# Part of an MLP's second product moved behind the scheduled stage, and a tail of Strassen products in place of the output projection

## The chip, the cores and the metric

The kernel runs on one core of one Trainium2 chip. The metric is the device time of one execution in microseconds. A core has a matrix engine (TensorE, PE in the profile; its weight loads are PEld), VectorE (DVE), ScalarE (ACT), GpSimd (POOL) and SyncE (SP, which only issues DMAs here). Each runs its own list of instructions in order and waits on semaphores for the others.

## The reference

One token block of S = 2048 rows and D = 1024 columns; 32 heads of width 32; an MLP of 3584 inner columns.

```python
xn = layernorm(x)
q, k, v = split(xn @ wqkv)                       # 32 heads of 32
p = softmax(q @ k.T * 32 ** -0.5)                # 2048 x 2048 for each head
s = concat(p @ v) @ wo
h = xn @ w1 + b1                                 # 2048 x 3584
act = h * tanh(log1p(exp(-abs(h))) + max(h, 0))  # mish
g = silu(act @ w2)
out = x + s * g
```

All is f32. The outer products with weights are computed in TensorE's fp32r form: each operand is split into a high part and a low part (the rest), and a product is three matmuls, high by high, high by low, low by high (`THREE`). The split is an ACT copy to the high part (`copy`, L288) and a subtraction for the low part (`low`, L296).

## The kernel before

It has three stages.

1. Layer norm, transposes, v, and q and k. The q/k product is already done by Strassen's scheme: 7 products of half-size blocks in place of 8, with sums of blocks made on the vector engines (L798). Up to about 519 us.
2. The scheduled stage, to about 3179 us. Streams of operations (`t_stream`, `s_stream`, `h_stream`, `y_stream`, `p_stream`) give each operation an engine, a cost, a key (its due time, from `due`, `SLOW` and `UNTIL`) and what it takes from rings of buffers and PSUM banks. `Plan` lays them out one after another in a list scheduler, and that order is the order in which the instructions are written. The string `LEAN` chooses, stretch by stretch, which kinds lean forward. Numbers in it only set the order.
   For each of the 32 heads: the scores q·k are computed twice, once for their row maxima (`s`, L920, reduced on DVE, L926), once with the maximum in the contraction, for exp (`t`, L1007, then ACT, tile `p`, 128x2048 for each of 16 key tiles). The product p·v is made in groups of 6, 5 and 5 key tiles (`pv`, L1054). The denominators are a chain on POOL: 15 adds of 128x2048 into one tile `z` (L1036). After the last add, four column blocks of `z` are summed over the partitions by matmuls with ones (`zp`, L1080), and ACT and DVE make the reciprocal and scale the head's output, which is stored to `ot` in DRAM. The next head's `z` chain starts when the `zp` of the head before has read its `z`.
   Beside it runs the MLP, over 4 chunks of 512 rows and 28 inner tiles of 128 columns: `h` (L1213), mish on ACT and DVE (the operations `d1` to `d7`, `a1` to `a5`; `a5` and `d7` are the split of the activation), and the second product `y` (L1303), in blocks of two inner tiles (`YB`), whose partial results DVE adds into `yacc` (L1325). A chunk's `yacc` is stored to `ys`. The weights w2 are split once (ACT and POOL), kept in DRAM (`w2s`) and reloaded for each chunk.
3. The output projection, `op` (L1402): 768 matmuls, 16 row tiles x 2 halves x 8 x 3. `p_stream` prepares its weights (`wo`, in pieces of 128x1024) and first inputs within the scheduled stage; the first half of the sums for the first four row tiles is planned as the end of that stage. Each result is multiplied by silu(y) and added to x on DVE (L1495, L1496).

Of the kernel before, what the change touches and what calls it, by code (L numbers as in the profile page):

```python
# [40 lines left out]
PS, ACTS, W2S, Y0, Y1 = 7, 3, 5, 0.6, 0.17  # L41
# [11 lines left out]
LEAN = ("11875111088588544715468766661886741604280263056046486663654100588"  # L53
        "24308444562028442608686254255866647666488105044664767708017872000")
# [176 lines left out]
def body(ctx: ExitStack, tc: tile.TileContext, x, wqkv, wo, w1, b1, w2, out):  # L231
# [23 lines left out]
    ys = [dram.tile([P, 4, D], F32, name=f"ys{i}") for i in range(NC)]  # L255
    zeros = dram.tile([DH, S], F32R, name="zeros")
# [638 lines left out]
    total = 2 * 4 * NS * MM + NC * FT * 48 * MM + NS * PV  # L895
# [332 lines left out]
    def mish(n, made, t):  # L1228
# [51 lines left out]
        o5 = op("DVE", 0.69, need=[o4], emit=d5, give=[("d", p2), ("b", p2)], kind="mish")  # L1280
        o6 = op("DVE", 0.69, need=[o5, o3], emit=d6, give=["r"], kind="mish")
# [3 lines left out]
    w2_took, w2_uses, w2_ends = {}, {}, {}  # L1285
    yacc = mlp.tile([P, 4, D], F32, name="yacc")

    def y_stream():
        for m in range(W2S):
            w2_op(m, [m_there[0, 3]])  # L1290
        for B in range(NC * FT // YB):
            c, b = divmod(B, FT // YB)
            done = []
            for dh in range(2):
                for s in range(4):
                    t = {}
                    for j in range(YB):
                        n, m_ = YB * B + j, (B * 2 + dh) * YB + j
                        for i, (p, q) in enumerate(THREE):
# [10 lines left out]
                            due = YB * B + YB + Y0 + g * Y1 + (BEHIND if B >= NC * FT // YB - 2 else 0)  # L1310
# [6 lines left out]
                            if s == 3 and i == 2 and m_ + W2S < NC * FT * 2:  # L1317
                                w2_op(m_ + W2S)
# [9 lines left out]
            if b == FT // YB - 1:  # L1328
# [6 lines left out]
    wt, ohl, ps, wo_loads, wo_ops, o_ops, o_first = {}, {}, {}, {}, {}, {}, []  # L1335
    raws_ = {}

    def in_p(name):
        return lambda at: att.tile([P, S], F32, tag=f"p{at['p']}", name=name)

    def raw_op(name, halves, tile_of, loads, **kw):

        done = []
        for i, (n, src, from_) in enumerate(loads):
            def emit(at, i=i, n=n, src=src):
                if i == 0:
                    raws_[name] = tile_of(at)
                w = S // halves
                raws_[n] = raws_[name][:, i * w:(i + 1) * w]
                nc.sync.dma_start(raws_[n], src)  # L1350
            if i:
                kw = dict(need=done[:1])
            done.append(op("SP", 0.1, emit=emit, bytes_=P * S * 4 // halves,
                           **{**kw, "need": list(kw.get("need", ())) + from_}))
        return done

    def wo_raw(name, ks, tile_of, **kw):
        a = raw_op(name, 2, tile_of, [(("wo", k), wo[k * P:(k + 1) * P, :], []) for k in ks], **kw)
        for k, o in zip(ks, a):
            wo_loads[k] = o  # L1360

    def wo_op(k, where, eng, **kw):
        def high(at):
            wt[k] = where()
            copy(wt[k][:, 0], raws_["wo", k])

        def rest(at):
            low(nc.gpsimd if eng == "POOL" else nc.vector, wt[k][:, 1], raws_["wo", k], wt[k][:, 0])

        need = kw.pop("need", [])  # L1370
        a = op("ACT", 1.05, need=[wo_loads[k]] + need, emit=high, **kw)
        wo_ops[k] = op(eng, 2.36 if eng == "POOL" else 1.3, need=[a], emit=rest, key=2 * total if eng == "POOL" else None,
                       both=eng == "DVE")

    def o_raw(name, ks):
        a = raw_op(name, 4, in_p(name), [(("o", k), ot[k][:, 0:512], [stored[h] for h in range(4 * k, 4 * k + 4)])
                                         for k in ks], take=["p"])
        for k, o in zip(ks, a):
            o_op(k, o)

    def o_op(k, load):
        def high(at):
            if k % HK == 0:
                xts_.setdefault(NC, []).append(chunk("xo0", k // HK))
            ohl[0, k] = xts_[NC][k // HK][:, :, k % HK]
            copy(ohl[0, k][:, 0], raws_["o", k])

        a = op("ACT", 0.6, need=[load] + ([o_first[k // HK]] if k % HK else []),
               take=[] if k % HK else [f"xc{k // HK}"], emit=high)
        if k % HK == 0:  # L1390
            o_first.append(a)
        o_ops[k] = op("DVE", 0.69, need=[a], both=True,
                      emit=lambda at: low(nc.vector, ohl[0, k][:, 1], raws_["o", k], ohl[0, k][:, 0]))


    BANKS, bank_of = ("s", "s", "t", "t", "y", "y", "z", "o"), {}
# [8 lines left out]
    def p_stream():  # L1405
# [23 lines left out]
        while "h" not in final:  # L1429
            yield None  # L1430
# [130 lines left out]
```

## Time and profile before

| | |
|---|---|
| time, median of 3 runs | 3362.5 us (3362.36 to 3362.78) |
| span of the profiled execution | 3358.0 us |
| TensorE busy | 3345.8 us, 100% of the span |
| VectorE / ScalarE / GpSimd busy | 2510.8 / 2056.5 / 2524.7 us |
| matmuls of `y` (L1303) | 2688 |
| matmuls of `op` (L1402) | 768, in 174.11 us at the end |
| adds of `z` on POOL | 448 of 4615 ns and 32 of 4628 ns |

The time of a run is 4.5 us above the span of the profiled execution (3362.5 against 3358.0). The profile's page gives busy times by engine; groups of instructions by line; the chain of waits that ends last; and a timeline. TensorE's clock is full in all 40 slices of the span. A line number is that of the kernel before; lines in the changed kernel are 6 higher in the first parts (`low` is L302, the `z` add L1042, `zp` L1086), the tail's matmul is L1528 there, and its sums are L1375 (weights), L1414 (activations) and L1533 (results).

### The profile page before, as it was taken

How to read it: one execution, taken by the hardware profiler on the slowest of the kernel's cores; microseconds unless marked ns; L12 is line 12 of the kernel's file. 1: busy time of each engine (PE TensorE's matmuls, PEld its weight loads, DVE VectorE, ACT ScalarE, POOL GpSimd, SP SyncE). 2: the span in 40 equal slices, each digit the busy share in tenths (PEclk: the TensorE clock that was granted, in tenths of full speed). 3: DMA queues.
4: the chain of work that ended last, by engine and by line, in shares of the span. 5: the costliest groups of instructions: out<-in, count | busy, mean ns of one | idle time of the engine just before them, and what ended most of it. 6: DMA issues, size and time to landing. Idle time of an engine off the chain costs nothing.

```text
span 3358.0 us, 45795 instructions
## 1 busy us (share of the span) xinstructions
PE 3345.8 (100%) x16886; PEld 2458.4 (73%) x16886; DVE 2510.8 (75%) x3987; ACT 2056.5 (61%) x3313; POOL 2524.7 (75%) x750
## 2 busy tenths in 40 slices
PE   9999999999999999999999999999999999999999
PEld 7888887776777677776777677777677777767787
DVE  6665678877877778887888688888787888886542
ACT  5233436676766666666676666666667666667621
POOL 1323546999999887888888988888888898889800
PEclk9999999999999999999999999999999999999999
DMA  7865745454565643343335334333344433433482
GB/s 248 298 204 181 242 146 183 140 184 152 169 191 172 221 126 115 105 122 114 101 117 179 111 101 126 101 112 116 101 151 139 116 106 112 130 108 107 140 304 83
DMA packets 291460, 501.56 MB, mean 149 GB/s; under 512 B 88138, under 2 KB 151114, under 8 KB 269130
## 3 DMA queue, kind: packets, MB, share of 16 engines
q1 hardware_dynamic: 271524, 456.95, 43.8%
q10 hardware_dynamic: 19712, 41.69, 3.3%
q8 instruction: 133, 2.18, 0.3%
q14 instruction: 91, 0.75, 0.1%
HBM read 352.55 MB, written 144.97 MB: 148 GB/s over the span
## 4 chain that ended last, share of the span: by engine, by line
PE 96%; DMA 1%; DVE 1%; POOL 1%; issue 0%; ACT 0%; SPq 0%; ACTq 0%; POOLq 0%; DVEq 0%
PE y L1303 18%; PE h L1213 18%; PE t L1007 14%; PE s L920 13%; PE pv L1054 13%; PE op L1402 5%; PE v L354 5%; PE q_y L798 3%; PE q_z L798 2%; PE q_x L798 2%; PE zp L1080 1%; PE s L700 0%; POOL z L1036 0%; PE pt L423 0%; DMA w2r<-in_B_w_dram 0%
## 5 line engine op out<-in xcount | busy, mean ns | idle before, releaser
L1036 POOL TENSOR_TENSOR z<-z,p 128x2048 f32<-128x2048 f32 x448 | 2067.7, 4615 | 98.0 <-ACT p L285 72.9
L285 ACT ACTIVATE p<-t,zero 128x512 f32<-128x512 f32 x2048 | 1377.1, 690 | 560.1 <-PE t L1007 535.7
L926 DVE TENSOR_REDUCE mx<-s 128x1 f32<-128x512 f32 x1984 | 1322.3, 685 | 382.7 <-PE s L920 371.9
L1303 PE MATMUL y<-w,act 128*128 128x512 f32 x2688 | 920.3, 391 | 0.8 <-DVE yacc L1325 0.5
L1007 PE MATMUL t<-qstack,kstack 128*128 128x512 f32 x2048 | 799.1, 393 | 1.1 <-ACT p L285 0.7
L920 PE MATMUL s<-kstack,qstack 128*128 128x512 f32 x1984 | 772.6, 393 | 0.2 <-ACT p L285 0.2
L1213 PE MATMUL h<-xr,w 128*128 128x512 f32 x2016 | 697.7, 391 | 0.4 <-DMA xr<-xs 0.4
L1303 PEld LDWEIGHTS y<-w,act 128*128 128x128 f32 x2688 | 503.3, 188 | 114.3 <-issue 6.7
L1007 PEld LDWEIGHTS t<-qstack,kstack 128*128 128x128 f32 x2048 | 383.8, 188 | 114.8 <-issue 18.0
L1054 PE MATMUL pv<-p,v 128*32 128x512 f32 x4096 | 459.3, 594 | 0.0
L920 PEld LDWEIGHTS s<-kstack,qstack 128*128 128x128 f32 x1984 | 369.6, 188 | 118.5 <-issue 32.1
L1213 PEld LDWEIGHTS h<-xr,w 128*128 128x128 f32 x2016 | 378.3, 188 | 81.2 <-issue 3.4
L1325 DVE TENSOR_TENSOR yacc<-yacc,y 128x512 f32<-128x512 f32 x416 | 282.7, 680 | 82.6 <-PE y L1303 81.5
L1054 PEld LDWEIGHTS pv<-p,v 128*32 128x32 f32 x4096 | 123.3, 110 | 282.7 <-issue 281.1
L1036 POOL TENSOR_TENSOR z<-p,p 128x2048 f32<-128x2048 f32 x32 | 148.1, 4628 | 185.2 <-PE zp L1080 146.6
L1213 PE MATMUL h<-xc,w 128*128 128x512 f32 x672 | 231.3, 391 | 1.3 <-DMA w<-w1s 1.0
L354 PE MATMUL v<-vw,xc 128*128 128x512 f32 x768 | 179.7, 392 | 1.2 <-ACT xc L288 0.7
L354 PEld LDWEIGHTS v<-vw,xc 128*128 128x128 f32 x768 | 142.7, 188 | 32.0 <-ACT xc L288 1.4
L1213 PEld LDWEIGHTS h<-xc,w 128*128 128x128 f32 x672 | 125.9, 188 | 30.5 <-issue 2.5
L288 ACT ACTIVATE act<-h 128x512 fp32r<-128x512 f32 x112 | 66.6, 595 | 88.2 <-DVE h L1262 87.0
L798 PE MATMUL q_y<-xc,wq 128*128 128x512 f32 x480 | 115.3, 389 | 0.0
L798 PEld LDWEIGHTS q_y<-xc,wq 128*128 128x128 f32 x480 | 90.0, 188 | 18.8
(149 smaller groups left out, 2947.4 us busy)
## 6 DMA issues: line engine op xcount, KB each, us to landing
w<-w1s SPq DMA_DIRECT2D x91, 1024.0 KB, 5.4
w<-w2s SPq DMA_DIRECT2D x168, 512.0 KB, 4.0
w2s<-w SPq DMA_DIRECT2D x56, 512.0 KB, 4.0
qstack<-qs SPq DMA_DIRECT2D x96, 256.0 KB, 6.3
kstack<-ks SPq DMA_DIRECT2D x96, 256.0 KB, 5.8
w1s<-w SPq DMA_DIRECT2D x21, 1024.0 KB, 5.8
qs<-qst ACTq DMA_DIRECT2D x32, 512.0 KB, 4.1
ks<-qst ACTq DMA_DIRECT2D x32, 512.0 KB, 3.7
```

The source lines that it names most:

```text
L285: nc.scalar.activation(out_, in_, fn, bias=zero if bias is None else bias, scale=scale)
L354: nc.tensor.matmul(ps, xc[t // 4][k // HK][:, a, k % HK, (t % 4) * P:(t % 4 + 1) * P], vw[i, k // 2][:, b, k % 2], start=n == 0, stop=n == ...
L798: nc.tensor.matmul(ps, w[:, a, k], xx[:, b, k], start=m == 0 and i in (0, 1, 4), stop=m == 3 * HK - 1, skip_group_check=i not in (0, 1, 4))
L920: nc.tensor.matmul(sp_, qst[h % 3][:, qt * P:(qt + 1) * P], kst[h % 3][:, kc * 512:(kc + 1) * 512], start=True, stop=True)
L926: nc.vector.reduce_max(tiles["mx"][:, qt, kc:kc + 1], tiles[qt, kc], axis=AX.X)
L1007: nc.tensor.matmul(tp, kst[h % 3][:, kt * P:(kt + 1) * P], qst[h % 3][:, c * 512:(c + 1) * 512], start=True, stop=True)
L1036: nc.gpsimd.tensor_tensor(zs[h], pts[T - 1] if kt == 1 else zs[h], pts[T], ALU.add)
L1054: nc.tensor.matmul(pv[h][c * DH:(c + 1) * DH, :], vt[h][:, k, :], pts[T - kt + k][:, c * 512:(c + 1) * 512], start=k == 0, stop=k == NT - 1)
L1213: nc.tensor.matmul(t["h"], w1t[n][:, a, k], xts_[c][k // HK][:, b, k % HK], start=i == 0, stop=i == 3 * KT - 1)
L1303: nc.tensor.matmul(t["y"], acts[n][:, p, s * P:(s + 1) * P], w2t[m_][:, q], start=j == 0 and i == 0, stop=j == YB - 1 and i == 2)
L1325: nc.vector.tensor_tensor(ya, ya, t["y"], ALU.add)
L1402: nc.tensor.matmul(ps[t, dh], ohl[t // 4, k][:, a, s * P:(s + 1) * P], wt[k][:, b, r], start=k == 0 and i == 0, stop=k == KT - 1 and i == 2)
```

## The change

Eight of the 28 inner tiles (2, 5, 8, 11, 16, 19, 22, 25; `DEFER`) leave `y`. Their activations are not split but stored to DRAM (`ats`) by SP (`put`), after a mish that ends in `d6_`. `y` then runs over the 20 that are left, 10 blocks of two (`BLOCKS`). After the scheduled stage there is a tail of 16 jobs: eight "y" jobs make the share of the deferred tiles, for 256 rows each, and eight "o" jobs make the output projection for 256 rows each. Every job is a product of a 256x1024 by a 1024x1024 block by Strassen's scheme (Winograd's form): 7 products of half-size blocks (`mm7`), 12 matmuls each. The weights' four quarters b11, b12, b21, b22 (tiles `yb0` to `yb3` and `ob0` to `ob3`, 128x2048) give sums T1 to T4 and, split in high and low, seven units `yu0` to `yu6` (for the o jobs `ou0` to `ou6`). A job's inputs (`araw`) give sums S1 to S4 on POOL (in job 0 S1 and S2 on DVE) and seven units `a<job>_0` to `a<job>_6` of 128x512. Three PSUM banks x, y, z of a job take products 0 and 2, 1, 3 and 5, 4 and 6; `e<job>_0` is a copy of product 0 (ACT), that must be taken before product 2 is added to the same bank; `e<job>_1` and `e<job>_3` are DVE sums. "y" jobs add to `ys`, take silu and store to `gs`; "o" jobs load `gs` and x.

`tail_stream`, the last stream of the scheduled stage, loads the quarters into the buffers of the heads' stacks as these come free, and makes T3, T2, T4 and the lows of `yu0`, `yu1`, `yu2` on POOL and the first a-unit. The costs and order constants change too: `SLOW` 1.25 to 1.08, `Y1` 0.17 to 0.25, and another `LEAN`.

```diff
-SLOW, UNTIL = 1.25, 700.0
-W2_Q = 0
+SLOW, UNTIL = 1.08, 700.0
+DEFER = (2, 5, 8, 11, 16, 19, 22, 25)
+KEPT = [f for f in range(FT) if f not in DEFER]
+BLOCKS = [KEPT[i:i + 2] for i in range(0, len(KEPT), 2)]
+NB = len(BLOCKS)
+NP = NT // 2
...
+        if n % FT in DEFER:
+            o6 = op("DVE", 0.69, need=[o5, o3], emit=d6_, give=[("d", t["own"]), ("b", t["own"]), "h"], kind="mish")
+            put_ops[n] = op("SP", 0.1, need=[o6], emit=put, give=["r"], bytes_=P * 512 * 4)
+            return
...
-        for B in range(NC * FT // YB):
-            c, b = divmod(B, FT // YB)
+        for B in range(NC * NB):
+            c, b = divmod(B, NB)
...
+    def tail_stream():
...
+        b11, b12 = load(0, final[H - 3]), load(1, final[H - 3])
...
+        b21, b22 = load(2, final[H - 2]), load(3, final[H - 2])
+        t3 = sum_("T3", [b12, b22])
...
+        u0 = split(0, [b11, final["h"]], ["xc0"])
+        t2 = sum_("T2", [u0, t3])
+        u1 = split(1, [t2, final["h"]], ["xc1"])
+        u2 = split(2, [b21, final["h"]], ["w1", "w1"])
+        t4 = sum_("T4", [u2, t2])
...
-    plan.run([t_stream(), s_stream(), h_stream(), y_stream(), p_stream()])
+    plan.run([t_stream(), s_stream(), h_stream(), y_stream(), tail_stream()])
...
+    SOURCE = (0, 0, 2, 1, 0, 2, 3)
+    KEYS = ("x", "y", "x", "y", "z", "y", "z")
...
+    def mm7(j, i):
...
+        for k in range(HK):
+            for a, b in THREE:
+                nc.tensor.matmul(ps, units[j, i][:, a, k], units[set_, i][b][:, k], start=m == 0 and i in (0, 1, 4),
+                                 stop=m == 3 * HK - 1, skip_group_check=i not in (0, 1, 4))
...
+    a_load(1, raw_tile(1))
+    for which, eng in (("S1", nc.vector), ("S2", nc.vector), ("S3", nc.gpsimd)):
+        a_sum(0, which, eng, small(f"0{which}", which))
+    b_sum("y", "T1", nc.gpsimd)
+    b_high("y", 3)
...
+    for j in range(last + 1):
+        for i in range(7):
+            mm7(j, i)
+            nxt = j + 1
+            if j == 0:
+                if i < 6:
+                    a_unit(0, i + 1)
+                if i == 0:
+                    b_low("y", 3, nc.vector)
+                if 0 < i < 4:
+                    b_unit("y", i + 3)
+            later.tick()
+            after(j, i)
+            if j == NP - 1:
+                if i == 3:
+                    b_sum("o", "T4", nc.gpsimd)
+                if i == 4:
+                    b_sum("o", "T1", nc.gpsimd)
+                b_unit("o", i)
+                if i == 0:
+                    b_sum("o", "T2", nc.vector)
+            if nxt <= last:
+                if i == 1:
+                    for which in ("S1", "S2", "S3"):
+                        a_sum(nxt, which, nc.gpsimd, small(f"{nxt}{which}", which))
+                later.at(LAG, lambda nxt=nxt, i=i: a_unit(nxt, i))
...
+            if i >= 4:
+                for n in {4: (4,), 5: (2, 5), 6: (6,)}[i]:
+                    done(j, n)
```

`done` makes the piece's end: for "y" a POOL add of e, a DVE add from PSUM and silu; for "o" two POOL operations (e times g, then into x) and two on DVE. `b_unit` and `a_unit` are an ACT copy and a DVE low; `a_unit` of product 2 is followed by S4 on POOL.

The order at three places. A row is line, operation, output, inputs and shape; names carry the head or the job and a running number. First POOL at the end of the scheduled stage, in head 31's chain of adds (`z31`). Before:

```order
L1036 TENSOR_TENSOR z31_29501<-z31_29501,p509_29909 128x2048
L1036 TENSOR_TENSOR z31_29501<-z31_29501,p510_29947 128x2048
L1036 TENSOR_TENSOR z31_29501<-z31_29501,p511_29984 128x2048
L296 TENSOR_TENSOR wo4_30066<-wr2_30007,wo4_30066 128x1024
L296 TENSOR_TENSOR wo6_30177<-wr3_30146,wo6_30177 128x1024
```

And now (`yu0_0`, `yu1_1`, `yu2l` are the units' tiles, L302 their lows; `yb0<-yb1,yb0` is T2, `yb2<-yb2,yb0` is T4):

```order
L302 TENSOR_TENSOR yu0_0_28597<-yb0_27443,yu0_0_28597 128x2048
L1042 TENSOR_TENSOR z31_28295<-z31_28295,p506_28561 128x2048
L1375 TENSOR_TENSOR yb0_27443<-yb1_27447,yb0_27443 128x2048
L1042 TENSOR_TENSOR z31_28295<-z31_28295,p507_28591 128x2048
L302 TENSOR_TENSOR yu1_1_28785<-yb0_27443,yu1_1_28785 128x2048
L1042 TENSOR_TENSOR z31_28295<-z31_28295,p508_28673 128x2048
L302 TENSOR_TENSOR yu2l_28615<-yb2_28144,yu2h_28614 128x2048
L1042 TENSOR_TENSOR z31_28295<-z31_28295,p509_28704 128x2048
L1375 TENSOR_TENSOR yb2_28144<-yb2_28144,yb0_27443 128x2048
L1042 TENSOR_TENSOR z31_28295<-z31_28295,p510_28728 128x2048
L1042 TENSOR_TENSOR z31_28295<-z31_28295,p511_28758 128x2048
```

Five operations of the tail have moved in between the adds; before, what belonged to the next stage stood behind them.

TensorE at the same place, around head 31's `zp`. Before:

```order
L1054 MATMUL pv31_29644<-p511_29984,v31_29343 32x512 x4
L1080 MATMUL zp31_30139<-z31_29501,ones_162 32x512 x4
L1303 MATMUL y55_1_2_30108<-w2_223_30042,act111_30040 128x512
L1303 MATMUL y55_1_3_30156<-w2_222_29991,act110_29875 128x512 x3
L1303 MATMUL y55_1_3_30156<-w2_223_30042,act111_30040 128x512 x3
L1402 MATMUL op0_0_30165<-wo0_28707,xo0_0_30050 128x512 x3
```

And now:

```order
L1319 MATMUL y39_1_3_28833<-w2_159_28751,act111_28753 128x512 x3
L1060 MATMUL pv31_28425<-p507_28591,v31_28138 32x512 x4
L1060 MATMUL pv31_28425<-p508_28673,v31_28138 32x512 x4
L1060 MATMUL pv31_28425<-p509_28704,v31_28138 32x512 x4
L1060 MATMUL pv31_28425<-p510_28728,v31_28138 32x512 x4
L1060 MATMUL pv31_28425<-p511_28758,v31_28138 32x512 x4
L1086 MATMUL zp31_28870<-z31_28295,ones_174 32x512 x4
L1528 MATMUL op0_x_28902<-yu0_0_28597,a0_28821 128x512 x12
L1528 MATMUL op0_y_28921<-yu1_1_28785,a0_1_28915 128x512 x12
```

The last `y` now stands ahead of `zp31`, and the first thing behind it is the tail.

DVE within the last stage. Before, in the middle of the projection (`ohl` is a split input, `y3` and `x3` the end of a piece):

```order
L296 TENSOR_TENSOR ohl3_2_30781<-oraw3_2_30782,ohl3_2_30781 128x512
L1495 TENSOR_TENSOR y3_9_30585<-op9_0_30870,y3_9_30585 128x512
L1496 TENSOR_TENSOR x3_9_30583<-x3_9_30583,y3_9_30585 128x512
L296 TENSOR_TENSOR ohl3_3_30784<-oraw3_3_30785,ohl3_3_30784 128x512
L1495 TENSOR_TENSOR y3_9_30585<-op9_1_30899,y3_9_30585 128x512
```

And now, from job 7 to job 8 (`ou` are the o jobs' units, `ob0<-ob1,ob0` is T2):

```order
L302 TENSOR_TENSOR a7_4_29888<-7S1_29771,a7_4_29888 128x512
L302 TENSOR_TENSOR ou0_0_29893<-ob0_29114,ou0_0_29893 128x2048
L1375 TENSOR_TENSOR ob0_29114<-ob1_29250,ob0_29114 128x2048
L302 TENSOR_TENSOR a7_5_29910<-araw7_29675,a7_5_29910 128x512
L1533 TENSOR_TENSOR e7_1_29914<-op7_y_29897,e7_0_29891 128x512
L302 TENSOR_TENSOR ou1_1_29916<-ob0_29114,ou1_1_29916 128x2048
L302 TENSOR_TENSOR a7_6_29938<-araw7_29675,a7_6_29938 128x512
L302 TENSOR_TENSOR ou2l_29942<-ob2_29386,ou2h_29941 128x2048
L302 TENSOR_TENSOR a8_0_29957<-araw8_29810,a8_0_29957 128x512
L1533 TENSOR_TENSOR e7_3_29960<-op7_y_29897,e7_0_29891 128x512
L302 TENSOR_TENSOR ou3_29963<-ob1_29250,ou3_29963 128x2048
```

The weights of the second half of the tail are prepared on DVE between the steps of job 7, four times as long each as the pieces before.

More of the change, by code (lines that the diff above doesn't have):

```diff
@@ L1332, in y_stream @@
         final["y"] = m
[L1335 to L1393, printed above, removed]
@@ L1396, in body @@
[L1396 to L1412 removed]
+    weights, units, araw, asum = {}, {}, {}, {}
@@ new lines, in a_src, with a_high, a_low, load @@
+    def a_src(j, i):
+        return part(j, *((0, 0), None, (0, 1), None, None, (1, 1))[i]) if i in (0, 2, 5) else asum[j, {1: "S2", 3: "S3", 4: "S1", 6: "S4"}[i]]
+    def a_high(j, i, tile_):
+        units[j, i] = tile_
+        copy(tile_[:, 0], a_src(j, i))
+    def a_low(j, i, eng):
+        low(eng, units[j, i][:, 1], a_src(j, i), units[j, i][:, 0])
+    first = {}
+    def tail_stream():
+        far = 2 * total
+        def load(part_, need):
+            return op("SP", 0.1, need=[need], emit=lambda at: b_load("y", part_), bytes_=P * S * 4)
+        def sum_(which, need):
+            return op("POOL", 4.61, need=need, emit=lambda at: b_sum("y", which, nc.gpsimd), key=far)
+        def split(i, need, take):
+            h_ = op("ACT", 1.9, need=need, emit=lambda at: b_high("y", i), take=take)
+            return op("POOL", 4.61, need=[h_], emit=lambda at: b_low("y", i, nc.gpsimd), key=far)
```

296 lines of the change are left out of this document (182 added, 114 removed).

## The prediction

> **What bounds the kernel now.** I read the page first: its busy shares and its chain of waits.
>
> ```profile
> PE 3345.8 (100%) x16886; PEld 2458.4 (73%) x16886; DVE 2510.8 (75%) x3987; ACT 2056.5 (61%) x3313; POOL 2524.7 (75%) x750
> PE 96%; DMA 1%; DVE 1%; POOL 1%; issue 0%; ACT 0%; SPq 0%; ACTq 0%; POOLq 0%; DVEq 0%
> PE y L1303 18%; PE h L1213 18%; PE t L1007 14%; PE s L920 13%; PE pv L1054 13%; PE op L1402 5%; PE v L354 5%; PE q_y L798 3%; PE q_z L798 2%; PE q_x L798 2%; PE zp L1080 1%; PE s L700 0%; POOL z L1036 0%; PE pt L423 0%; DMA w2r<-in_B_w_dram 0%
> ```
>
> TensorE carries 96% of the chain, so a matmul fewer is worth its full time as long as TensorE keeps being fed. Next the same by stretches of time (columns: start:end, length, then busy time of PE, PEld, DVE, ACT, POOL, granted clock, DMA share, GB/s): the Strassen q/k stage, the middle of the scheduled stage, its last head.
>
> ```profile
> 320.00:500.00 180.00, 179.21 (x791) 147.82 (x790) 130.67 (x194) 68.36 (x126) 85.30 (x61) 1.00 0.64 202
> 2250.00:2500.00 250.00, 250.00 (x1302) 178.00 (x1299) 203.31 (x324) 168.54 (x265) 217.81 (x51) 1.00 0.39 115
> 3098.00:3177.00 79.00, 79.00 (x431) 55.09 (x419) 45.75 (x60) 55.56 (x87) 73.22 (x16) 1.00 0.33 109
> ```
>
> TensorE has no gap at full clock. The engine with least room beside it is POOL, 217.81 of 250 (87%) in the middle and 73.22 of 79 in the last head. The timeline of POOL shows why, for one head in the middle and for the last one (columns: start, length, engine, line, operation; in brackets how long the engine had been idle and on whom it waited):
>
> ```profile
> 1752.89 4.63 POOL L1036 TENSOR_TENSOR z<-p,p 128x2048 f32<-128x2048 f32 x1 [5.73 <-PE zp L1080]
> 1757.59 37.39 POOL L1036 TENSOR_TENSOR z<-z,p 128x2048 f32<-128x2048 f32 x8
> 1795.11 28.07 POOL L1036 TENSOR_TENSOR z<-z,p 128x2048 f32<-128x2048 f32 x6
> ...
> 3100.40 4.62 POOL L1036 TENSOR_TENSOR z<-p,p 128x2048 f32<-128x2048 f32 x1 [5.54 <-PE zp L1080]
> 3105.10 66.82 POOL L1036 TENSOR_TENSOR z<-z,p 128x2048 f32<-128x2048 f32 x14
> 3171.89 2.83 POOL L296 TENSOR_TENSOR wo<-wr,wo 128x1024 fp32r<-128x1024 f32 x1
> ```
>
> And TensorE's at both ends of the last head:
>
> ```profile
> 3099.15 1.04 PE L1080 MATMUL zp<-z,ones 128*32 128x512 f32 x8
> ...
> 3172.07 4.50 PE L1054 MATMUL pv<-p,v 128*32 128x512 f32 x40
> 3176.39 1.04 PE L1080 MATMUL zp<-z,ones 128*32 128x512 f32 x8
> 3177.36 1.90 PE L1303 MATMUL y<-w,act 128*128 128x512 f32 x7
> 3179.10 5.17 PE L1402 MATMUL op<-wo,xo 128*128 128x512 f32 x22
> ```
>
> A head's sum is a chain of 15 POOL adds, 1752.89 to 1823.18 = 70.3 us, that begins when the head before has done its zp matmuls and that this head's zp matmuls wait for. After the last zp TensorE goes on without a gap.
>
> **The matmuls.** The prices (columns: count, busy us, mean ns), and the chain's rows of one pv group and of the whole projection:
>
> ```profile
> L1036 POOL TENSOR_TENSOR z<-z,p 128x2048 f32<-128x2048 f32 x448 | 2067.7, 4615 | 98.0 <-ACT p L285 72.9
> L296 POOL TENSOR_TENSOR w<-w2r,w 128x512 fp32r<-128x512 f32 x56 | 72.5, 1295 | 32.6 <-ACT w L288 32.6
> L296 DVE TENSOR_TENSOR ohl<-oraw,ohl 128x512 fp32r<-128x512 f32 x16 | 10.7, 687 | 19.2 <-ACT ohl L288 17.8 <-DMA x<-in_A_x_dram 1.4
> L288 ACT ACTIVATE ohl<-oraw 128x512 fp32r<-128x512 f32 x16 | 9.7, 622 | 39.4 <-DVE x L1496 39.4
> L288 ACT ACTIVATE wo<-wr 128x1024 fp32r<-128x1024 f32 x8 | 8.3, 1054 | 15.5 <-DMA wr<-in_A_wo_dram 9.6 <-DVE wo L296 5.9
> L285 ACT ACTIVATE y<-y,zero 128x1024 f32<-128x1024 f32 x16 | 18.3, 1142 | 31.3 <-DVE x L1496 31.2
> 3036.71 5.29 PE pv L1054 x48
> 3179.26 174.11 PE op L1402 x768
> ```
>
> The projection's 768 matmuls take 174.11 us, 0.2267 each. The second product loses 8 of 28 inner tiles: 4 chunks x 8 tiles x 4 row tiles x 2 halves x 3 = 768 fewer. The tail is 16 jobs x 7 products x 12 = 1344 where 768 stood. So 192 fewer in all: **-43.5 us**. The y additions (DVE, 128 fewer), the ACT and DVE steps that split 32 activations, and fewer w2 loads go too; the 32 stores of activations and the loads of w2 parts come (DMA share 0.39). None of these stands on the chain of waits before, and I cost both at nothing; TensorE covers them.
>
> **The last head, the largest wait.** In the changed order five 128x2048 operations of the tail (three lows, T2, T4) stand between head 31's adds; in the old one nothing did. TensorE has between zp30 and zp31 235 matmuls x 0.2267 = 53.3, 128 pv matmuls x 0.110 (5.29/48) = 14.1 and zp 1.0, together 68.4. POOL needs 70.3 + 5 x 4.615 = 93.4 (before: 71.5 against 77). Everything behind zp31 on TensorE is the tail, and there is nothing else to run: 93.4 + 0.3 - 67.4 = **+26** (28 if adds take the 4.77 of the last head, 66.82/14; 20 if the first add need not wait the 5.54 that it waited for the zp of the head before). T3 stands in the gap ahead of the chain and costs nothing as long as that gap of 5.5 us is there.
>
> **The other heads.** Early heads have 10 to 12 weight lows among the adds: 70.3 + 12 x 1.295 = 85.8, and their TensorE work falls, by the order's counts, to 83.5 to 87.8. Two of heads 1 to 5 come out over it, by 3.6 and 2.9: **+6** (0 to 12). From head 7 a typical one has 265 matmuls, 60.1 + 14.1 + 1.0 = 75.2, against 70.3 + about 1.3 to the next first add; it stays TensorE's, with 3.6 us of slack where there were 6 (275 matmuls before). I take 0 there; the upper end is a rival.
>
> **The tail's preparation.** The old projection's parts were split in pieces of 512 and 1024, and its first ones ahead of the stage's end. The tail splits 128x2048 units on DVE: four in job 0 and all seven of the second set in jobs 7 and 8. A 128x1024 low alone took 1.21 (below), a 128x512 one 0.69, so 128x2048 is about 1.21 + 2 x 0.52 = 2.2; on ACT 1.05 + 2 x 0.43 = 1.9. The price depends on POOL, too. DVE's timeline at the end of the stage, and POOL's at the same time:
>
> ```profile
> 3160.73 1.66 DVE L296 TENSOR_TENSOR wo<-wr,wo 128x1024 fp32r<-128x1024 f32 x1
> 3162.32 0.67 DVE L1325 TENSOR_TENSOR yacc<-yacc,y 128x512 f32<-128x512 f32 x1
> ...
> 3164.83 2.62 DVE L296 TENSOR_TENSOR xo<-or,xo 128x512 fp32r<-128x512 f32 x1
> 3171.65 4.22 DVE L296 TENSOR_TENSOR xo<-or,xo 128x512 fp32r<-128x512 f32 x3
> 3175.80 1.21 DVE L296 TENSOR_TENSOR wo<-wr,wo 128x1024 fp32r<-128x1024 f32 x1
> ```
>
> ```profile
> 3151.97 19.95 POOL L1036 TENSOR_TENSOR z<-z,p 128x2048 f32<-128x2048 f32 x4
> ```
>
> While POOL adds, a DVE operation with both inputs in SBUF took 2.62 for 0.69, one with an input in PSUM 0.67 as always, and POOL's four adds 4.99 each for 4.62. So the two engines take turns, and the tail's lows, all SBUF, must be added to POOL's work and not laid beside it.
>
> Job 0: after zp31 come ln and exp (ACT) and two steps of the norm (DVE), 0.62 to 0.69 each, S1 and S2, then the low of unit 3, T1 on POOL (4.62), and on it unit 4 (1.9 + 2.2); units 5 and 6 follow on DVE, and their a-lows behind each. Last a0_6's low is done 33.5 us after zp31 where its product could start at 17.2 + 0.9; that is about 15, and 2 to 3 more in job 1, where e1_0's copy stands behind two silu on ACT. With no turns it is 9. I take **+17** (9 to 19), since the rows show turns.
>
> Jobs 7 to 8: from the first product of job 7 to the second silu the two engines have 8 DVE operations of 2.2, 7 lows of 0.69, T4 and T1 of 4.62 and 8 small POOL ones of 1.3: 17.6 + 4.8 + 9.2 + 10.4 = 42, with the silu and e8_0's copy 44. Product 8,2 waits for that copy, which is due 2 x 2.72 after job 7's 19.05, 21.8 after that start: 22 late, plus some 8 where unit 1 waits for T2, unit 4 for T1 and ACT's order binds them. **+28** (22 with no turns, since DVE alone has 27 us and the line through T2, T4, T1 remains; 30 above).
>
> Steady jobs: 7 products are 84 x 0.2267 = 19.05. An o job has on POOL 10 x 1.295 and on DVE 11 x 0.69, 20.5 in turns: 1.5 over, seven times. A y job has 7 x 1.3 + 7 x 0.69 = 13.9, hidden, and up to 1 us for the copy behind a silu. **+13** (2 to 22).
>
> The Trainium skill's page "SBUF — State Buffer", section "SBUF: two separate sides", says that the shared port is an exclusive lock for any GpSimd operation against a two-SBUF-input DVE one. Here only long POOL operations show it; by that rule the steady term is 11 of the 13 and stays, by the rows alone it could be 2.
>
> **The end.** After the last matmul of before, and at its very start:
>
> ```profile
> 3353.40 0.69 DVE L1495 TENSOR_TENSOR y<-op,y 128x512 f32<-128x512 f32 x1 [3.95 <-PE op L1402]
> 3354.12 0.69 DVE L1496 TENSOR_TENSOR x<-x,y 128x512 f32<-128x512 f32 x1
> 3354.84 0.34 SPq L1498 DMA_DIRECT2D out_dram<-x  x1
> 1.82 7.14 PE L473 MATMUL idle<-xc 128*128 128x512 f32 x19 [1.82 <-POOL xc L470]
> ```
>
> Now POOL's product and addition of the piece before (1.3 each) and both DVE ones queue there: **+4** (0 to 5). The last row is a start after idling: 0.376 a matmul for 0.2267. Behind the 26 us wait that is at most 19 x 0.149 = 2.8; it falls into job 0, where the preparation is late anyway, so 0 (0 to 3). The Trainium skill's "TensorE: Matmul & The Clock Gate", section "What's actually happening", has the clock halved after an idle window of about 3.4 us; it would put the same 0 to 3 behind each of two waits.
>
> **Sum.** -43.5 + 26 + 6 + 17 + 28 + 13 + 4 = +50.5 on the profiled span of 3358.0: 3408.5. The runs (median 3362.5) lie 4.5 above the span: **3413**.
>
> **Rivals.** *Dense tail, faster:* the tail could run like the q/k stage, of the same form, which kept TensorE busy 179.21 of 180 with DVE at 130.67. Then the preparation terms fall to some 2 and the sum is -43.5 + 26 + 6 + 4 + 2 = -5.5: 3357, and 3345 with the last head at 20 and the early heads at 0. It decides from tail waits under 7.5 (43.5 - 26 - 6 - 4). Against it speak the 2.62 row and the 27 us of DVE work that jobs 7 and 8 get at once. *No turns:* if short operations don't block each other, 9 + 22 + 2 = 33 for 58: 3388. For it: the 1.66 row, only 0.45 over 1.21. *POOL bounds the scheduled stage:* if the gap of 5.73 between a head's last and the next first add stays, a head takes 76.0 against 75.2 and less (heads 7 to 30 lie between 70.6 and 75.2), some 1.7 x 24 = 41 more: 3454. Against it: the pv group in that gap waits for ACT and not for POOL, so it runs ahead once POOL is late.
>
> **How the numbers follow.** Forecast 0.50, no turns 0.24, dense tail 0.14, POOL-bound 0.12. The range reaches from 3372, the no-turns case with its smaller ends, to 3445, the forecast with all upper ends (2 + 6 + 2 + 2 + 9 + 1 + 3 = 25) and a part of the POOL-bound case; the dense tail and half the last are left out. A difference of 0.2% (6.7 us) is about what a measurement can tell: faster 0.10 and within it 0.04, the dense tail's two ends, and slower 0.86, the rest.
>
> **What would show it.** A wait of 20 to 28 us of zp on z ahead of the tail, with the tail's operations among POOL's last adds; waits of product 0,3 to 0,6 on DVE; the largest wait of the tail at 8,2 on ACT; o jobs of 20.5 us; lows of 128x2048 over 3 us beside T4 and T1. Wrong it would be if the five operations cost the last head nothing, or if jobs 8 on stay at 19.05 throughout.

## The result, and the profile after

The changed kernel takes 3457.69 us (median of 4, 3456.28 to 3459.94) against 3362.44: ratio 1.0282, interval 1.0268 to 1.0297. It is 95 us slower. The sign was forecast; the size was not, 3457.7 lies above the range's 3445. The profiled span is 3458.1 against 3358.0, so 100.1 us are to be found where the sum had 50.5. That is 5 more than the runs differ, because the profiled execution of the changed kernel is the longest of its four (spans 3454.5 to 3458.1) and that of the kernel before is a short one: where time and span are of one execution, the time is 1.8 to 3.0 above the span, not 4.5.

The page's busy times of the changed kernel, and one of its waits (engine, line, whom it waited for: total, times, longest):

```profile
PE 3351.7 (97%) x16694; PEld 2428.6 (70%) x16694; DVE 2581.3 (75%) x3973; ACT 2090.9 (60%) x3367; POOL 2743.5 (79%) x874
PE zp L1086 <- POOL z L1042: 24.4, 1, 24.4
```

There are 192 matmuls fewer, and yet TensorE is busy no less: it now runs with gaps, and in places at a lower clock (0.50 granted from 3062 to 3085, for one). POOL has 219 us more. To find the place, the span is cut at two points that both kernels have, the zp of head 0 (zp0) and the zp of head 30 (columns as before: start:end, length, then busy PE, PEld, DVE, ACT, POOL, clock, DMA). First before, then after:

```profile
617.30:3099.20 2481.90, 2479.65 (x12901) 1762.75 (x12897) 1968.44 (x3126) 1695.07 (x2701) 2195.92 (x572) 1.00 0.43 131
```

```profile
618.90:2987.30 2368.40, 2344.09 (x12174) 1627.14 (x12170) 1868.53 (x2969) 1657.85 (x2654) 2174.64 (x555) 1.00 0.42 126
```

This stretch has 723 matmuls fewer (the rows' counts differ by 727, with zp matmuls at the cuts), worth 163.9 us, and became only 113.5 shorter: **50 us lost in heads 1 to 30**, where the sum had 6. TensorE's idle time there went from 2.3 to 24.3. The rest doesn't show as idle, because the records of pipelined matmuls, 0.39 each at a pitch of 0.2267, overlap: 59 starts (pv and zp left aside) lie over 0.45 us apart, 6 before, and hold together 37 us above the pitch, 3 before. The granted clock takes a small part; it was below full in heads 5, 10 and 23 alone (0.98, 0.98, 0.96). Taken by heads (from zp to zp, less their price: 0.2267 for each matmul, 14.1 for pv and 1.0 for zp) heads 1 to 6 have 32.6 over their matmuls' price, 9.0 before, and heads 7 to 30 have 48.8, 22.1 before: 24 and 27 lost. Ten of the 27 are in head 23.

The last head, POOL (part of its rows) and TensorE:

```profile
3030.69 4.63 POOL L302 TENSOR_TENSOR yu<-yb,yu 128x2048 fp32r<-128x2048 f32 x1
3035.26 4.63 POOL L1042 TENSOR_TENSOR z<-z,p 128x2048 f32<-128x2048 f32 x1
3039.83 4.65 POOL L1375 TENSOR_TENSOR yb<-yb,yb 128x2048 f32<-128x2048 f32 x1
...
3071.87 9.05 POOL L1042 TENSOR_TENSOR z<-z,p 128x2048 f32<-128x2048 f32 x2
```

```profile
3052.05 4.50 PE L1060 MATMUL pv<-p,v 128*32 128x512 f32 x40
3080.98 1.93 PE L1086 MATMUL zp<-z,ones 128*32 128x512 f32 x8 [24.43 <-POOL z L1042]
```

The chain took 92.3 us (2988.58 to 3080.92), and TensorE stood 24.4 at zp31. The tail by stretches: jobs 0 and 1; 2 to 5; 6 to 8; 9 to the last matmul:

```profile
3081.00:3137.70 56.70, 47.44 (x176) 35.17 (x177) 40.02 (x36) 22.15 (x27) 31.07 (x17) 0.87 0.36 135
3137.70:3215.90 78.20, 77.83 (x337) 62.37 (x336) 46.57 (x52) 26.18 (x40) 43.55 (x29) 1.00 0.54 202
3215.90:3304.90 89.00, 65.36 (x254) 51.71 (x253) 59.38 (x48) 33.81 (x39) 45.83 (x25) 0.87 0.34 118
3304.90:3449.00 144.10, 135.66 (x589) 109.62 (x587) 96.28 (x110) 29.11 (x51) 99.58 (x69) 1.00 0.53 192
```

Against 19.05 a job: jobs 0 and 1 took 31.6 and 23.3 (+16.8), jobs 7 and 8 39.3 and 28.6 (+29.8), jobs 2 to 6 99.3 (+4.1), jobs 9 to 15 20.5 to 20.6 each and 20.8 for the last (+10.7).

### The profile page after: what moved, and what is told of

It reads as the page before. It is cut to its first block, busy times and chain, and to the rows that moved or that the text cites. A ratio compares the mean times of both kernels' runs of the same rounds, so it can differ in the third digit from the quotient of the medians.

```text
span 3458.1 us, 45768 instructions
## 1 busy us (share of the span) xinstructions
PE 3351.7 (97%) x16694; PEld 2428.6 (70%) x16694; DVE 2581.3 (75%) x3973; ACT 2090.9 (60%) x3367; POOL 2743.5 (79%) x874
## 5 line engine op out<-in xcount | busy, mean ns | idle before, releaser
L291 ACT ACTIVATE p<-t,zero 128x512 f32<-128x512 f32 x2048 | 1358.3, 690 | 308.3 <-PE t L1013 271.3
L1219 PE MATMUL h<-xr,w 128*128 128x512 f32 x2016 | 686.3, 392 | 4.1 <-DMA xr<-xs 3.9
L1319 PE MATMUL y<-w,act 128*128 128x512 f32 x1920 | 672.2, 394 | 3.0 <-DVE yacc L1341 1.5
L1319 PEld LDWEIGHTS y<-w,act 128*128 128x128 f32 x1920 | 361.5, 189 | 84.0 <-DVE yacc L1341 3.2
L1341 DVE TENSOR_TENSOR yacc<-yacc,y 128x512 f32<-128x512 f32 x288 | 195.8, 680 | 47.7 <-PE y L1319 47.0
L291 ACT ACTIVATE e<-e,zero 128x512 f32<-128x512 f32 x112 | 80.5, 719 | 92.5 <-DVE e L1239 92.5
L294 ACT ACTIVATE act<-h 128x512 fp32r<-128x512 f32 x80 | 47.8, 597 | 99.4 <-DVE h L1268 97.2
```

What stands on the lines that cost most here:

```text
L291: nc.scalar.activation(out_, in_, fn, bias=zero if bias is None else bias, scale=scale)
L294: nc.scalar.activation(out_, in_, AF.Copy, scale=scale)
L1219: nc.tensor.matmul(t["h"], w1t[n][:, a, k], xts_[c][k // HK][:, b, k % HK], start=i == 0, stop=i == 3 * KT - 1)
L1319: nc.tensor.matmul(t["y"], acts[n][:, p, s * P:(s + 1) * P], w2t[m_][:, q], start=j == 0 and i == 0, stop=j == YB - 1 and i == 2)
L1341: nc.vector.tensor_tensor(ya, ya, t["y"], ALU.add)
```

## The experiments

The first question was what holds heads 1 to 30. Theory A: POOL's chain, at run time. Theory B: other faults of the new order.

**1. Shorter adds in the same order.**

```diff
-            nc.gpsimd.tensor_tensor(zs[h], pts[T - 1] if kt == 1 else zs[h], pts[T], ALU.add)
+            w = slice(0, 64 if kt in (5, 10) else S)
+            nc.gpsimd.tensor_tensor(zs[h][:, w], (pts[T - 1] if kt == 1 else zs[h])[:, w], pts[T][:, w], ALU.add)
```

> Changed kernel, same order, but 2 of the 15 adds of every head's z chain (the 5th and the 10th) work on 64 of 2048 columns; that leaves part of the denominators out. Each chain is 9.2 us shorter. Theory A (POOL's chain plus the 5.7 us to the next one paces the scheduled stage): heads 1 to 30, 50.5 us over the kernel before in waits, lose 35 to 50, and the last head's wait 9: 3400 to 3415. Theory B (the new order itself starves TensorE, by s behind DVE and by loads): only the last head's 9 us go: 3447 to 3451.

3451.55 us. The stretch from zp0 to zp30, and POOL at head 10 of this kernel:

```profile
619.40:2983.60 2364.20, 2344.76 (x12178) 1629.38 (x12174) 1868.53 (x2969) 1657.46 (x2654) 1918.58 (x555) 1.00 0.42 127
```

```profile
1389.47 33.50 POOL L1043 TENSOR_TENSOR z<-z,p 128x2048 f32<-128x2048 f32 x9
1424.07 23.40 POOL L1043 TENSOR_TENSOR z<-z,p 128x2048 f32<-128x2048 f32 x5 [1.10 <-ACT p L291]
1461.45 4.63 POOL L1043 TENSOR_TENSOR z<-p,p 128x2048 f32<-128x2048 f32 x1 [13.98 <-PE zp L1087]
```

POOL lost 256 us of work and waits 14 for zp; heads 1 to 30 became 4 us shorter in all, no more than single runs differ (experiment 6). As it was put, theory A fell: while the kernel runs, POOL is not what TensorE waits for in those heads. Left was an order that is itself too long, for whatever reason. The last head's wait fell by 3.9 (to 20.5) and not by the 9 of both theories, since POOL now waits there for ACT (3.2 for a unit of the tail, 1.4 for `p`).

**2. Shorter adds, and the order made for them.** The planner lets the last pv group of a head wait for the head's last add (`need.append(adds[T])`), and zp follows it. If the planned POOL chain (70.3 and then pv, zp and the hand-over, 5.7) is longer than the TensorE work that is left, the planner spaces the matmuls by it, and TensorE, which runs in order, keeps that spacing even when POOL is early. Theory A' is this; the control is the same edit on the kernel before. The bias in the edit's last line is for sums that are left out in part, whose logarithm could be infinite; it adds no instruction.

```diff
-            nc.gpsimd.tensor_tensor(zs[h], pts[T - 1] if kt == 1 else zs[h], pts[T], ALU.add)
+            w = slice(0, S) if kt == 1 else slice(0, 1536) if kt % 2 else slice(512, S)
+            nc.gpsimd.tensor_tensor(zs[h][:, w], (pts[T - 1] if kt == 1 else zs[h])[:, w], pts[T][:, w], ALU.add)
-        adds[T] = op("POOL", 4.61, need=exps[T] + (exps[T - 1] if kt == 1 else [adds[T - 1]]), emit=emit,
+        adds[T] = op("POOL", 4.61 if kt == 1 else 3.5, need=exps[T] + (exps[T - 1] if kt == 1 else [adds[T - 1]]), emit=emit,
-            act(t["r"], t["z"], AF.Ln)
+            act(t["r"], t["z"], AF.Ln, bias=one)
```

> Changed kernel with every add of z but a head's first on 1536 of 2048 columns, and the planner told so (3.5 us instead of 4.61), so that the order is made anew for a shorter chain; a quarter of the sums is left out. Theory A' (POOL's chain and the 5.7 us behind it set the order at the planning, and the order then holds TensorE whether POOL is late or not): heads 1 to 30 lose 35 to 50 us; the last head's wait has 14 x 1.1 less, 15: 3393 to 3410. Theory B (other faults of the new order): heads 1 to 30 the same within 10, only the 15 of the last head: 3433 to 3453.

> The kernel before with the same two edits, the control. Both theories: its heads are TensorE's own, so nothing to win: 3355 to 3378, the upper part if another order is a little worse.

3398.04 us and, for the control, 3373.19. From zp0 to zp30, the changed kernel with shorter adds and then the control:

```profile
606.10:2932.70 2326.60, 2323.75 (x12189) 1629.54 (x12185) 1881.34 (x2979) 1669.08 (x2661) 1709.65 (x556) 1.00 0.43 129
```

```profile
614.70:3102.80 2488.10, 2482.78 (x12892) 1760.37 (x12888) 1968.60 (x3129) 1690.64 (x2700) 1731.24 (x571) 1.00 0.43 130
```

The stretch fell from 2368.4 to 2326.6 with 14 more matmuls in it (3.2 us): 45 of the 50 us came back, and TensorE's idle time went from 24.3 to 2.9. By heads it is all of the 24 of heads 1 to 6 and 20 of the 27 of heads 7 to 30. The control rose by 6. A new order alone doesn't do it: the control of experiment 3, planned anew with adds of full length, took 2368.9. Where the time was lost is seen in TensorE's own waits from 600 to 2980 (total, times, longest), after and then with shorter adds and a new order:

```profile
PE s L926 <- DVE mx L932: 9.1, 17, 1.7
PE h L1219 <- DMA xr<-xs: 3.9, 1, 3.9
```

```profile
PE s L926 <- DVE mx L932: 0.4, 1, 0.4
```

In the changed kernel's order there are runs of `s` matmuls ahead of a head's last pv group, put where the plan had nothing else to do, and they wait for DVE's maxima: 32 of the 59 starts that are over 0.45 us apart are theirs, with 20 of the 37 us. So A' is shown for 45 of 50 us by experiments 1 and 2 together: shorter adds alone gave 4 at most, shorter adds with a plan made for them gave 45. Neither run shortens the chain in the plan alone, or takes the tie of pv to the last add away, so that this very tie does it is read in the code and not shown by a run. The last 5 us are no more than profiles of one order differ: five that have the same order in these heads (the changed kernel and experiments 4, 5, 6 and 8) took 2361.9 to 2368.4. One wait for a load in head 23 is part of that (3.9 at 2441 here; from 2437 to 2456 the granted clock was 0.82).

**3. Two z buffers.** They take the wait for zp out of the chain. Room came from w2's buffers, with a control for that.

```diff
-PS, ACTS, W2S, Y0, Y1 = 7, 3, 5, 0.6, 0.25
+PS, ACTS, W2S, Y0, Y1 = 7, 3, 3, 0.6, 0.25
...
-    for name, n in (("b", 7), ("s", S_B), ("t", T_B), ("d", D_B), ("o", 1), ("p", PS), ("z", 1), ("e", 1), ("r", 1), ("on", 1),
+    for name, n in (("b", 7), ("s", S_B), ("t", T_B), ("d", D_B), ("o", 1), ("p", PS), ("z", 2), ("e", 1), ("r", 1), ("on", 1),
```

> Changed kernel with two z buffers (room from 3 instead of 5 buffers of w2), so that a head's chain need not wait for the zp of the head before; everything is planned anew. Theory A: the floor of a head falls from 76.0 to 70.3 plus lows, heads 1 to 30 lose 25 to 45: 3413 to 3433. Theory B: within 10 of 3458.

> Changed kernel with 3 instead of 5 buffers of w2 and one z buffer, planned anew: the control for the run with two. Both theories: 3448 to 3475, since a reload of w2 takes 4 us and a buffer is used for 12 matmuls.

3585.64 us, and 3457.84 for the control. The stretch with two buffers:

```profile
615.60:3123.90 2508.30, 2414.53 (x12371) 1674.08 (x12363) 1921.53 (x3022) 1687.81 (x2682) 2178.77 (x561) 0.99 0.41 123
```

From head 2 on every chain now begins 14 to 30 us ahead of the zp before it, as meant, and the order is much worse: 94 us of idle, 197 more matmuls spent by head 30, and heads 30 and 31 left with 198 and 54 where 265 are usual. Both theories' numbers missed; the control fell within its own. It looks as if a plan with one wait less spent early the matmuls that fill gaps, but no run shows that. This run says nothing on A' and is a warning that each new order brings its own error.

**4. The five operations of the last head, on DVE.**

```diff
-            return op("POOL", 4.61, need=[h_], emit=lambda at: b_low("y", i, nc.gpsimd), key=far)
+            return op("DVE", 2.3, need=[h_], emit=lambda at: b_low("y", i, nc.vector), key=far)
...
-            return op("POOL", 4.61, need=need, emit=lambda at: b_sum("y", which, nc.gpsimd), key=far)
+            eng, cost, e = ("POOL", 4.61, nc.gpsimd) if which == "T3" else ("DVE", 2.3, nc.vector)
+            return op(eng, cost, need=need, emit=lambda at: b_sum("y", which, e), key=far)
```

> Changed kernel, with the three lows, T2 and T4 that stand between head 31's adds given to DVE (2.2 us each instead of 4.6). If DVE's two-SBUF-input operations and POOL take turns, the chain is still 5 x 2.2 = 11 longer than 15 adds and the wait of zp31 falls from 24.4 to about 12: 3445. If they run side by side, it falls to 1 or 2: 3435. If the wait had another cause than these five, 3458.

3444.29 us. POOL, DVE (part of its rows) and TensorE of this kernel:

```profile
2987.39 75.04 POOL L1042 TENSOR_TENSOR z<-z,p 128x2048 f32<-128x2048 f32 x14
```

```profile
3018.55 3.78 DVE L302 TENSOR_TENSOR yu<-yb,yu 128x2048 fp32r<-128x2048 f32 x1
3029.48 6.02 DVE L302 TENSOR_TENSOR yu2l<-yb,yu2h 128x2048 fp32r<-128x2048 f32 x1
3043.19 5.49 DVE L1375 TENSOR_TENSOR yb<-yb,yb 128x2048 f32<-128x2048 f32 x1
```

```profile
3065.68 1.04 PE L1086 MATMUL zp<-z,ones 128*32 128x512 f32 x8
```

The chain is 79.8 us now, 9.5 over 70.3, close to 5 x 2.2 = 11: the two engines take turns, and each of DVE's five took 3.7 to 6.0. The wait of zp31 on POOL is gone, so these five operations are its cause. But TensorE's waits within this head, which were that one alone, are now others, ahead of zp31:

```profile
PE y L1319 <- DVE act L1281: 4.7, 1, 4.7
PE t L1013 <- DVE yacc L1341: 3.2, 1, 3.2
PE t L1013 <- ACT p L291: 3.0, 1, 3.0
```

So the head became 9.4 shorter (84.2 for 93.6) and not 24.4. The run is 13.4 faster and zp31 comes 15.3 earlier, but 5.9 of these stood at zp30 already, where the two kernels have the same instructions (experiment 6): that 3445 was forecast and 3444 came is in part luck.

**5. The o weights' T4 and T1 on DVE.** `b_sum("o", "T4", nc.gpsimd)` and T1's became `nc.vector`.

> Changed kernel with T4 and T1 of the o weights (jobs 7 and 8) on DVE instead of POOL. With turns between POOL and DVE the shared time falls by 2 x (4.6 - 2.2) = 4.8: 3451 to 3455. Side by side, DVE gets 4.4 more in the stretch where it is the longer one: 3458 to 3463.

3456.05 us. Jobs 7 and 8 took 64.8 for 67.9. That is 3.2 of the 4.8 that turns would give, and the other sign than side by side; in the time, 1.6 is less than single runs can tell. In these two jobs it is clear: they took 64.8 and, in experiment 9 with the same move, 64.7, but 67.6 to 68.5 in the profiles of the changed kernel and of experiments 4, 6 and 8. A wait moved: product 7,6 waits 2.61 on DVE for 8.43, and product 8,2 waits 10.90 on ACT for 6.88.

**6. Steady o jobs.**

```diff
+            w = slice(0, 512 if j < 10 else 32)
-            tt(G, e, e, g, ALU.mult)
-            tt(G, xx, xx, e, ALU.add)
+            tt(G, e[:, w], e[:, w], g[:, w], ALU.mult)
+            tt(G, xx[:, w], xx[:, w], e[:, w], ALU.add)
```

> Changed kernel with four of the ten POOL operations of each job from 10 to 15 on 32 of 512 columns (part of the result is left out). With turns, a job's 20.5 us of POOL and DVE fall to 16, so these jobs go to 19.05 and 6 x 1.5 = 9 go: 3449. If product 3's wait of 1.35 in each job is only the line of steps to it, it stays: 3455 to 3458 (the end may lose 3).

3442.61 us. Product 3 of job 11 in the changed kernel, and its like with the short operations:

```profile
3353.87 0.39 PE L1528 MATMUL op_x<-ou2h,a 128*128 128x512 f32 x1
3355.45 3.06 PE L1528 MATMUL op_y<-ou,a 128*128 128x512 f32 x12 [1.19 <-DVE e L1533]
```

```profile
3366.34 0.39 PE L1528 MATMUL op_x<-ou2h,a 128*128 128x512 f32 x1
3366.57 2.88 PE L1528 MATMUL op_y<-ou,a 128*128 128x512 f32 x12
```

From job 11 on every job takes 19.0, and the end after the last matmul fell from 9.1 to 6.1. So DVE's steps are late because of POOL's small operations, not for their own length. DVE's rows ahead of that product, in the changed kernel and with the short operations, show two ways in which they are:

```profile
3347.36 0.69 DVE L1533 TENSOR_TENSOR g<-op_y,g 128x512 f32<-128x512 f32 x1 [3.67 <-POOL e L1533]
3348.73 1.77 DVE L1533 TENSOR_TENSOR x<-x,g 128x512 f32<-128x512 f32 x1 [0.68 <-POOL x L1533]
3350.42 1.78 DVE L302 TENSOR_TENSOR a<-araw,a 128x512 fp32r<-128x512 f32 x1
```

```profile
3358.80 0.69 DVE L1533 TENSOR_TENSOR g<-op_y,g 128x512 f32<-128x512 f32 x1 [2.63 <-POOL e L1533]
3359.59 0.69 DVE L1533 TENSOR_TENSOR x<-x,g 128x512 f32<-128x512 f32 x1
3360.20 0.69 DVE L302 TENSOR_TENSOR a<-araw,a 128x512 fp32r<-128x512 f32 x1
```

Two operations of 0.69 took 1.77 and 1.78 beside POOL's, which are turns, 2.2 us in all; and DVE waits some 1.6 us less for POOL's results, which is the line of steps. The edit takes both away at once, so it doesn't say which of them the 1.5 us of a job are. The spans differ by 17.3: 7.7 in jobs 11 to 15, 3.0 at the end, and 6.2 ahead of zp31, where the two kernels have the same instructions. So single runs differ there by some 6 us, and differences of 1 to 6 us between single runs are not read as effects here.

**7. The lows of w1 and w2 on DVE.** Both `low(nc.gpsimd, ...)` and their planned operations became DVE's, at 0.75.

> Changed kernel with the lows of w1 and w2 (the 10 to 12 among the adds of heads 1 to 5) planned and run on DVE, nothing left out. If POOL's chain at the planning is what holds those heads, their floor falls by 13 to 16 each and the 24 us that heads 1 to 6 lost come back: 3433 to 3443. If DVE's turns with POOL cost the row maxima as much (each low waits up to 4.6 us for an add, 82 lows), TensorE waits for DVE in their place: 3450 to 3480.

3550.62 us, far above both. The two groups of lows, which take 1.30 on POOL:

```profile
L302 DVE TENSOR_TENSOR w<-w1r,w 128x512 fp32r<-128x512 f32 x42 | 98.1, 2336 | 1.1 <-ACT w L294 1.0
L302 DVE TENSOR_TENSOR w<-w2r,w 128x512 fp32r<-128x512 f32 x40 | 85.2, 2130 | 5.0 <-ACT w L294 4.8
```

DVE is busy 183 us with what it does alone in 0.69 x 82 = 57: the lows wait for POOL's adds, the row maxima stand behind them, and heads 1 to 6 came out 121 us over their matmuls' price instead of 33. Turns are shown again; on the early heads' share of A' this cannot speak, since DVE became the bound and the order is another one.

**8. The clock behind the last head's wait.** Matmuls of no use ahead of zp31, `nc.tensor.matmul(t["z"], last_p["p"][:, :P], last_p["p"][:, :512], start=True, stop=True)`, first 100 of them, then 27.

> Changed kernel with 100 matmuls of no use (22.7 us, on head 31's last p tile) ahead of the last zp, where TensorE waits 24.4 us: the clock is then granted in full at the tail's start. Theory A (the clock falls into waits that the preparation sets anyway): 3456 to 3459. Theory B (the half clock behind the wait costs by itself): 3 to 5 us less, 3453 to 3455.

> As the run before with 100, which kept TensorE for 86 us since each such matmul is two of 0.43 us, but with 27: 54 x 0.43 = 23 us, inside the 24.4 us that TensorE waits for the last zp. Theory A (the half clock behind that wait falls into job 0's own waits): 3455 to 3459. Theory B (it costs by itself): 3452 to 3454, by the 17 matmuls that ran at half clock up to 20 us behind zp31 (3.4 us).

3515.26 us with 100: I had their price wrong. They ran as 200 in 86.1 us (`p` is plain f32, and the pv matmuls on it are recorded twice as well), and pushed zp31 58 back. With 27 the wait is filled, and the clock granted from 3055 to 3082 was 1.00, where it had been 0.62:

```profile
3053.98 23.44 PE L1089 MATMUL zp<-p 128*128 128x512 f32 x54
3078.53 1.07 PE L1091 MATMUL zp<-z,ones 128*32 128x512 f32 x8 [1.11 <-POOL z L1042]
```

3455.58 us (3454.98 to 3457.27), ratio 1.0279 with 1.0262 to 1.0297, against 1.0282 with 1.0268 to 1.0297. The two can't be told apart. Jobs 0 and 1 took 53.3 for 54.9, but they took 53.3 in experiment 5 as well, which changes nothing there. The half clock behind that wait costs 2 us at most, as the sum's 0 to 3 had it.

**9. All three moves to DVE together** (4, 5 and 7).

> Changed kernel with all three moved to DVE: the lows of w1 and w2, the five operations among head 31's adds, T4 and T1 of the o weights; nothing left out. As the sum of the single parts (20, 14, 2): 3422 if they add; in no case under the kernel before, since the planned POOL chain of heads 7 to 30 (27), jobs 0, 1, 7, 8 (45) and the steady jobs (15) remain against 43.5 of matmuls.

3536.31 us (3530.81 to 3536.81), ratio 1.0518, 1.0501 to 1.0536. The 3422 is missed by far, since the 20 that it hoped for from the lows was a loss of 93 (experiment 7). It is 14.3 below experiment 7 alone, which is about what 4 and 5 gave, 13.4 and 1.6. No version here beats the kernel before; the shortest of the changed ones with nothing left out is experiment 4.

## Why the prediction was right or wrong

Term by term, in us (forecast; measured):

| step | forecast | measured |
|---|---|---|
| 192 matmuls | -43.5 | -43.5 |
| wait of the last head | +26 | +24.4 |
| heads 1 to 6 | +6 | +23.6 |
| heads 7 to 30 | 0 | +26.7 |
| jobs 0 and 1 | +17 | +16.8 |
| jobs 7 and 8 | +28 | +29.8 |
| steady jobs | +13 | +14.8 |
| end | +4 | +4.5 |
| sum | +50.5 | +97 |

The first row is a count times 0.2267 in both columns. Of the 3 us from 97 to 100.1, 1.6 lie ahead of zp0 (618.9 for 617.3).

**The step that failed is "The other heads".** It set a head's POOL floor (the least time that POOL needs from head to head) at 70.3 + 1.3 and found 3.6 us of slack against 75.2. POOL of the changed kernel, from head 10 to head 11:

```profile
1386.00 4.62 POOL L1042 TENSOR_TENSOR z<-p,p 128x2048 f32<-128x2048 f32 x1 [5.39 <-PE zp L1086]
1390.76 65.51 POOL L1042 TENSOR_TENSOR z<-z,p 128x2048 f32<-128x2048 f32 x14
1462.79 4.64 POOL L1042 TENSOR_TENSOR z<-p,p 128x2048 f32<-128x2048 f32 x1 [6.52 <-PE zp L1086]
```

The floor is 70.3 + about 5.7 = 76.0, and most of heads 8 to 30 took 75.6 to 76.4 from zp to zp, with 256 matmuls (73.1 of TensorE) as with 265 (75.2). The 265 were the most that such a head has and not the typical case; the mean price of heads 7 to 30 is 74.2. The early heads have the same error, 5.7 for 1.3 behind chains of 82 to 87. The rival "POOL bounds the scheduled stage" had the right floor and 41 us for heads 7 to 30. That is time over the matmuls' price, of which 48.8 were measured, but 22.1 of these stood there before: 27 lost, 50 with the early heads. It was given 0.12 on the argument that the pv group "runs ahead once POOL is late". While the kernel runs, that can be so: in the last head the pv group ran at 3052.05, 29 us ahead of zp31. But the plan ties that group to the last add, and experiment 1 shows that the order keeps its length with POOL early. The tie stands in a line of the kernel, `need.append(adds[T])`; the waits of a trace don't show it.

**The last head** was right in place, size and cause (experiment 4). **The turns of DVE and POOL** were right, and the case "no turns" is out: experiments 4 and 7 and the rows of experiment 6 show them. The rule of the Trainium skill's page "SBUF — State Buffer" ("SBUF: two separate sides") that was weighed in the steady term, an exclusive lock, which for a DVE operation with two SBUF inputs counts against a GpSimd operation that reads SBUF, agrees with the trace for small operations as well: in the steady o jobs DVE's lows of 0.69 took up to 1.78, and POOL's operations of 1.29 up to 1.74. That the o jobs took the 20.5 of the sum is luck, though. It counted eleven such DVE operations where a job has ten, and laid both engines' work end to end; in job 11 the records of both together cover 17.8 of the 20.57 us.

**Jobs 0 and 1** came out in size but in another place: job 0 was 12.5 late and job 1 4.2, for 15 and 2 to 3, and the largest wait was 4.16 at product 0,2, on DVE's low of its input, where 0,3 to 0,6 had been named.

**Jobs 7 and 8** came out in size, and in place in part. Three waits hold 21.9 of the 29.8: those of products 7,3 and 7,6, on DVE's e7_1 and e7_3 behind the new units, and that of 8,2 on ACT, which was forecast, but as the largest. The sum there has a slip: 2 x 2.72 after 19.05 is 24.5 and not 21.8, so its own terms make e8_0's copy 19.5 late and not 22. TensorE, DVE and POOL of the changed kernel:

```profile
3252.24 4.82 PE L1528 MATMUL op_y<-yu,a 128*128 128x512 f32 x12 [6.59 <-DVE e L1533]
3270.98 5.46 PE L1528 MATMUL op_z<-yu,a 128*128 128x512 f32 x12 [8.43 <-DVE e L1533]
3288.93 0.79 PE L1528 MATMUL op_x<-ou2h,a 128*128 128x512 f32 x1 [6.88 <-ACT e L294]
```

```profile
3259.24 6.10 DVE L302 TENSOR_TENSOR ou<-ob,ou 128x2048 fp32r<-128x2048 f32 x1
3265.26 4.97 DVE L302 TENSOR_TENSOR a<-8S,a 128x512 fp32r<-128x512 f32 x1
```

```profile
3258.20 11.49 POOL L1375 TENSOR_TENSOR ob<-ob,ob 128x2048 f32<-128x2048 f32 x2 [9.36 <-DVE ou2l L302]
```

A low of 0.69 took 4.97 beside T4 and T1, and e7_3 stood behind it.

**The dense tail** is out: jobs 0, 1, 7 and 8 alone lost 46.6. **The clock** cost nothing that could be told in the last head (experiment 8). The sum put it at 0 behind the other waits, too. There the twelve matmuls behind each of the three waits of jobs 7 and 8 took 4.82, 5.46 and 5.21 us for 2.88, at a granted clock of 0.50 (from 3250 to 3256, 3267 to 3276, 3287 to 3293.5). That is 6.9 of the 29.8; whether the preparation would have taken that time at full clock as well, no run shows.

Still open: whether the tie of pv to the last add is what makes the planned floor, since no run took it away, and how much of the early heads' 24 the weight lows alone would return, since experiment 7 made DVE the bound.

## What to carry to other kernels

When matmuls leave a stage that a scheduler has laid out, ask first which other engine's chain was just below TensorE's, and take its floor as the planner ties it, hand-overs included: here 76.0 against 75.2 plus about 0.8 of hand-overs on TensorE at the most, and less in every head with fewer matmuls. The order that was spaced by a slow chain kept its length when the chain got faster (experiment 1); the gain showed when the cost was cut in the plan too (experiment 2). Work that was moved from POOL to DVE here, with both inputs in SBUF and POOL busy, returned less than the difference of the prices (3.2 of 4.8 in experiment 5), and in experiment 7 it cost 93 us.

## What was not expected of the hardware

A 128x512 DVE low with both inputs in SBUF took 2.13 and 2.34 us on average beside a POOL chain, for 0.69 alone, over three times as long, and POOL does the same low in 1.30. A matmul of 128x128 by 512 on plain f32 tiles counted as two and took 0.86 us together (86.1 / 100), against 0.2267 for one in fp32r, so a filler of plain f32 is nearly four times as long as it looks. In head 10 of the changed kernel the granted clock was 0.50 for 3.4 us (1453.9 to 1457.3), though its records show no idle time of TensorE longer than 0.75 us in the 10 us before. So the clock was halved there without the idle window of about 3.4 us that the prediction speaks of.
